# The first two pairs of output blocks of a fused kernel's third matrix product also in seven half-products, their steps interleaved

## The chip, the cores and the metric

The kernel runs on one core of a Trainium2 chip. The metric is the device time of one execution in microseconds (us). TensorE (PE in the profile) multiplies matrices into PSUM banks, VectorE (DVE) and ScalarE (ACT) work elementwise, GpSimd (POOL) helps in the first stage, and SyncE (SP) issues the transfers.

## The reference, cut to what matters

An attention, then two feed-forward layers, all in float32, on 896 tokens (two batches of 448):

```python
x = attention(q, k, v)                                    # 896 x 768
h = np.maximum(np.maximum(x @ w1, x @ w2), x @ w3)        # w1, w2, w3: 768 x 768
y = h @ w_out                                             # 768 x 768
h2 = y @ w_in                                             # 768 x 2048
g = np.where(h2 > 0.0, h2, np.exp(np.minimum(h2, 0.0)) - 1.0)
out = g @ w_out2                                          # 2048 x 768
```

The change touches `y @ w_in`.

## The kernel before, in words

Everything is kept transposed: features on the 128 partitions, the 448 tokens of one batch along the free dimension. A weight block is 128 output columns wide and has six chunks of 128 rows. A float32 number is held as a high and a low part, so one chunk of one block for one batch takes three matmuls of 128x448: high weights by high data, high weights by low data, low weights by high data. A standard block is 2 batches x 6 chunks x 3 = 36 matmuls.

`unit` (called by name from the three matrix stages) does two neighbouring blocks f and f+1 in seven half-products (half of the chunks, one batch; 9 matmuls each) where the standard way has eight. It needs differences of the weights, named 13 and 24 in the program, and sums of the data, `sums_y` with q = 0 to 3, three chunks each. In the order of the code the products of a unit are called here:

- A: first half of block f's weights by the first three chunks of batch 0 (no sums)
- F: weights 13 by sums q=0, put aside as `s5` (function `out5`)
- Q1: weights 24 by sums q=1
- B: second half of block f's weights by the last three chunks of batch 0 (function `second`, no sums)
- Q2: weights 13 by sums q=2
- D: second half of block f+1's weights by sums q=3
- E: weights 24 by the last three chunks of batch 1 (no sums)

ScalarE copies the running PSUM bank aside at three points (`seed`, tiles pgs0, pgs1, pgs2), and VectorE adds `s5` to two of the four results (`added`). The weights reach a unit like this: SyncE loads a raw block (two buffers, `raw_wg`); ScalarE makes `top` (L194, one buffer); VectorE makes the float32 block `b_g` of raw and top (L196, one buffer `ub` for both blocks of a unit); VectorE forms 13 (`f13`, L760) and 24 (two half-size instructions, L777, in place); and `split` makes the high part on ScalarE (`hi`, L743) and the low part on VectorE (`lo`, L202) of each of 0, 13, 24 and 1. There are two buffers for 13 and 24 together (`ul`), and three (`w`) for 0 and 1. Each result then goes through `elu`: Relu and Exp on ScalarE (tile `e`), the join on VectorE (`gf`, L1019), and the split of g into a high part (ScalarE, L1024) and a low part (VectorE, L167).

Stage by stage: attention; h (tiles ph, p, ps); y in six standard blocks in the order `PY` (tiles py0, py1 for the two batches, L930 and L934); then w_in in 16 blocks (tiles pg): blocks 0 and 1 standard, the other seven pairs (2, 4, ... 14, `PG_UNITS`) as units one after the other in the order A, F, Q1, B, Q2, D, E; then out (tiles po). `y_block` splits y on ScalarE and VectorE (tiles x), and `y_sums` forms the sums of a chunk pair when both of its y blocks are there (VectorE steps `spare`, L978 and L990, and a split of each, tiles s and c).

The order of the instructions on each engine is written by a planner (`Plan.order` with `late_plan`): each task has an engine, an estimated cost and a due time `at`; the order in which TensorE's products are given is fixed by the code (`on_pe`), the other engines' order follows from the due times and the planner's estimates.

Of the kernel before, what the change touches and what calls it, by code (L numbers as in the profile page):

```python
# [8 lines left out]
F32 = mybir.dt.float32  # L9
# [11 lines left out]
B, H, S, D = 2, 12, 448, 64  # L21
# [19 lines left out]
PG_UNITS = (2, 4, 6, 8, 10, 12, 14)  # L41
PO_UNITS = (2,4,)
PO_CUT = 6
AWAY = 4
# [113 lines left out]
def fused_kernel(ctx: ExitStack, tc: tile.TileContext, qk, v, w1, w2, w3, wo, wi2, wo2, outT):  # L158
# [553 lines left out]
    def unit(name, src, lean, left, sums, leave, kind="p", base=0, stops=False):  # L712
# [76 lines left out]
        split("24", tk, "t", at + 2400, [t4, opened], slice(0, NK), [(u, name, 3)] if lean else [ut])  # L789
        split(1, None, "w", at + 9000, [full[1], ready["24"] if stops else None], dn, [(u, name, 3)])  # L790

        def product(ps, what, k, xs, after, q=None, gives=(), new=False):

            def run(eng):
# [12 lines left out]
                run, 9, [ready[what], *after] + ([sums.made[q, c] for c in range(HALF)] if q is not None else []),  # L807
# [24 lines left out]
        t5 = product(p, "13", 0, None, [], q=0, new=True)  # L832
        spare = "s5" if not lean else "best1" if kind == "po" else "ot"

        def out5(eng):
            pool, tag = {"s5": (pools.get("s5"), "s5"), "best1": (bp, "best1"), "ot": (pools.get("ot"), "ot")}[spare]
            s5.append(pool.tile([128, S], F32, tag=tag, name=f"s5_{name}"))
            nc.scalar.copy(s5[0], p[0])

        t5 = task(out5, "ACT", 530, clock[0] + 2000, [t5], takes=[spare], gives=["m"])  # L840
        yield
        t = product(a, "24", 0, None, [sb], q=1)
        sd = seed(a, d, t)
        yield
        if not stops:
            second()
            yield
# [150 lines left out]
    for f in PY:  # L998
        y_block(f, py_banks if PG_UNITS else None)
        if f >= HALF and PG_UNITS:  # L1000
            y_sums(f - HALF, py_banks)
# [46 lines left out]
    f = 0  # L1048
    while f < NF:
        if f in PG_UNITS:  # L1050

            def leave_g(k, b, ps, after, gives, at, more=None, frees=()):
                if more is not None:
                    after = [*after, added(ps, more, after, at, frees)]
                elu(f + k, b, ps, after, at, gives)

            list(unit(f"g{f}", [wi2[f], wi2[f + 1]], True, y, sums_y, leave_g, "pg"))
            f += 2
            continue
        parts, t = load(wi2[f], f"wi2_{f}", clock[0])  # L1060
        ps = [[] for _ in range(B)]

        def product(eng, chunks, ps=ps, parts=parts, f=f):
            if chunks[0] == 0:
                for b in range(B):
                    ps[b].append(psum(f"pg{f}_{b}"))
            multiply(ps, parts, y, 0, NK, True, True, chunks)
# [76 lines left out]
    f = 0  # L1144
# [68 lines left out]
```

## Time and profile before

| | |
|---|---|
| median of three runs | 459.61 us (459.44 to 460.14) |
| the profiled execution, its own time | 459.15 us |
| its span in the trace | 457.40 us |
| instructions | 6818 |
| TensorE matmuls | 2456 |
| busy: PE, DVE, ACT, POOL | 451.0, 349.0, 304.2, 43.0 us |

Busy time is the time in which an engine works on instructions. All times below are counted from the start of the span; 1.75 us of the execution's time lie outside it. A matmul's end is modelled (362 ns shown for each, while they start every 200 ns), so starts are what to read on TensorE.

### The profile page before, as it was taken

Reading aid. Unit: us, or ns where it says so; the run is one execution under the profiler, and the core shown is the slowest. Engines: PE = TensorE matmul, PEld = TensorE weight load, DVE = VectorE, ACT = ScalarE, POOL = GpSimd, SP = SyncE. Lnnn points to the kernel's source line nnn. Section 1 sums busy time; section 2 is a strip of 40 time slices with the busy share of each in tenths; the row PEclk is TensorE's granted clock in tenths of the full one; section 3 lists DMA queues with packets and bytes.
Section 4 is the critical chain, followed back from the end, with each engine's and each line's share of the span. In section 5 each row is a group of like instructions: output and inputs, shape, how many; then the busy total and the mean of one; then the engine's idle time right before and its main releaser. Section 6 shows DMA issues by size and latency. Waiting matters only on the chain.

```text
span 457.4 us, 6818 instructions
## 1 busy us (share of the span) xinstructions
PE 451.0 (99%) x2456; PEld 397.5 (87%) x2456; DVE 349.0 (76%) x696; ACT 304.2 (67%) x610; POOL 43.0 (9%) x93
## 2 busy tenths in 40 slices
PE   7999999999999999999999999999999999999996
PEld 3657657799999999999999999999999999999996
DVE  4999898589889994577689699999999797363201
ACT  5999897585666874354647799999995446443200
POOL 4665473000000000000000000000000000000000
PEclk9999999999999999999999999999999999999999
DMA  6463521244225531132341754233459425643002
GB/s 212 165 215 112 183 62 42 120 167 179 94 74 187 199 138 70 70 139 69 138 154 55 300 194 142 107 134 138 138 178 374 139 74 191 195 173 126 1 1 80
DMA packets 16273, 63.22 MB, mean 138 GB/s; under 512 B 1776, under 2 KB 3824, under 8 KB 16240
## 3 DMA queue, kind: packets, MB, share of 16 engines
q1 hardware_dynamic: 16240, 62.79, 39.5%
q8 instruction: 19, 0.31, 0.3%
q14 instruction: 14, 0.11, 0.1%
HBM read 56.36 MB, written 6.42 MB: 137 GB/s over the span
## 4 chain that ended last, share of the span: by engine, by line
PE 93%; DVE 2%; ACT 2%; DMA 1%; POOL 1%; issue 0%; SPq 0%; ACTq 0%
PE p L802 11%; PE pg00g L802 8%; PE ps L802 8%; PE py L930 6%; PE po L930 6%; PE pt L389 4%; PE o L412 4%; PE s L342 3%; PE py L934 3%; PE po L934 3%; PE pgs1g L802 3%; PE pgs0g L802 3%; PE pgs2g L802 3%; PE pg130g L802 3%; PE po00o L802 2%; PE ph L223 2%
## 5 line engine op out<-in xcount | busy, mean ns | idle before, releaser
L366 ACT ACTIVATE pr<-pr,nmx 128x384 f32<-128x384 f32 (+2 forms) x72 | 35.9, 504 | 4.4 <-DVE nmx L356 4.3
L930 PE MATMUL py<-h,hi_wo 128*128 128x448 f32 x144 | 34.6, 362 | 0.0
L194 ACT ACTIVATE top<-raw_wo 128x768 f16<-128x768 bf16 (+1 forms) x24 | 24.2, 1009 | 14.9 <-DMA raw_wo<-in_wo 9.2
L214 ACT ACTIVATE hi_wo<-f_wo 128x768 fp32r<-128x768 f32 (+1 forms) x20 | 15.7, 785 | 25.1 <-PE po00o L930 8.2
L379 POOL TENSOR_SCALAR pr<-pr,r 128x384 f32<-128x384 f32 (+2 forms) x60 | 29.6, 513 | 23.1 <-DVE r L375 12.5
L356 DVE CUSTOM_DVE_ANT_0 pr<-s,mask 128x384 f32<-128x384 f32 (+2 forms) x72 | 26.7, 414 | 6.3 <-PE s L342 6.1
L202 DVE SCALAR_TENSOR_TENSOR lo_wo<-f_wo,hi_wo 128x768 fp32r<-128x768 f32 (+1 forms) x20 | 17.5, 875 | 18.2 <-ACT hi_wo L214 18.0
L930 PEld LDWEIGHTS py<-h,hi_wo 128*128 128x128 f32 x144 | 27.0, 188 | 1.8
L342 PE MATMUL s<-qk 64*128 64x384 f32 (+3 forms) x192 | 26.6, 441 | 1.7 <-DMA qk<-in_qk 1.3
L342 PEld LDWEIGHTS s<-qk 64*128 64x128 f32 (+1 forms) x192 | 13.8, 172 | 11.8 <-DVE nmx L356 4.4
L802 PE MATMUL p<-s,hi 128*128 128x448 f32 x84 | 23.6, 362 | 0.0
L802 PE MATMUL ps<-x,hi 128*128 128x448 f32 x84 | 23.6, 362 | 0.0
L389 PE MATMUL pt<-ident,pr 128*128 128x128 f32 x144 | 22.0, 280 | 0.3 <-DVE l L370 0.2
L412 PE MATMUL o<-th,v 128*64 128x448 f32 (+2 forms) x144 | 22.0, 440 | 0.0
L815 ACT COPY ps<-p 128x448 f32<-128x448 f32 x21 | 10.9, 520 | 16.6 <-PE p L802 16.6
L389 PEld LDWEIGHTS pt<-ident,pr 128*128 128x128 f32 x144 | 15.9, 140 | 6.5 <-issue 2.3
L194 ACT ACTIVATE top<-raw_w 128x768 f16<-128x768 bf16 x18 | 19.5, 1083 | 2.1 <-DVE b L196 2.1
L934 PE MATMUL py<-h,lo_wo 128*128 128x448 f32 x72 | 20.2, 362 | 0.0
L194 ACT ACTIVATE top<-raw_wg 128x768 f16<-128x768 bf16 x14 | 15.2, 1085 | 7.5 <-issue 3.3
L802 PE MATMUL pg00g<-s,hi_g 128*128 128x448 f32 x70 | 19.7, 363 | 0.0
L196 DVE SCALAR_TENSOR_TENSOR f_wo<-raw_wo,top 128x768 int32<-128x768 int32 (+1 forms) x20 | 17.5, 874 | 2.4 <-ACT top L194 2.1
L1015 ACT ACTIVATE e<-e 128x448 f32<-128x448 f32 x32 | 18.6, 580 | 0.8
(286 smaller groups left out, 1335.8 us busy)
## 6 DMA issues: line engine op xcount, KB each, us to landing
raw_w<-in_w SPq DMA_DIRECT2D x18, 768.0 KB, 4.4
raw_wo<-in_wo SPq DMA_DIRECT2D x18, 768.0 KB, 4.4
raw_wg<-in_wi SPq DMA_DIRECT2D x14, 768.0 KB, 4.4
qk<-in_qk SPq DMA_DIRECT2D x11, 448.0 KB, 4.1
kept<-h SPq DMA_DIRECT2D x8, 448.0 KB, 2.6
v<-in_v SPq DMA_DIRECT2D x12, 256.0 KB, 3.1
raw_wo<-in_wo SPq DMA_DIRECT2D x6, 512.0 KB, 3.8
out_t<-ot SPq DMA_DIRECT2D x12, 224.0 KB, 2.0
```

The lines of the kernel that those rows point to most:

```text
L194: nc.scalar.mul(spread.bitcast(F16)[:, 1::2], top.bitcast(BF16), -1.0)
L196: nc.vector.scalar_tensor_tensor(out=f(), in0=below, scalar=13, in1=spread, op0=ALU.logical_shift_right, op1=ALU.bitwise_or)
L342: nc.tensor.matmul(out, us[e]["qk"][own, 0, C * i:w], us[e]["qk"][own, 1, :w], start=True, stop=True, skip_group_check=True)
L356: nc.vector.tensor_tensor_reduce(out=pr, in0=u["s", g][j or 0][:, at:at + w], in1=mask_r if i == NB else mask[:, FULL - w:], scale=-0.125, ...
L366: nc.scalar.activation(pr, pr, AF.Exp, bias=u["nmx"][:, n:n + 1], scale=-1.0, accum_out=u["l"][:, n:n + 1])
L379: engines[eng].tensor_scalar(out=u["pr", j, i], in0=u["pr", j, i], scalar1=u["r"][:, n:n + 1], scalar2=1.0, op0=ALU.mult, op1=ALU.mult)
L389: nc.tensor.transpose(pt[:e - C * c, at:at + C], u["pr", j if j is None else j ^ odd, i][:, C * c:e], ident)
L412: nc.tensor.matmul(u["o"][D * j:D * (j + 1), C * c:], u["v"][:, j, c], u["th_r"][:, j ^ odd] if c == NB else u["th"][:, c, j ^ odd, C * c: ...
L802: nc.tensor.matmul(ps[0], wt[:, HALF * kk + c], w[:, i, :], start=(new and c == m == 0), stop=(c == HALF - 1 and m == 2), skip_group_check ...
L930: nc.tensor.matmul(p[0], hi[:, c, :], xs[j][c0 + c][:, i, :], start=first and c == 0 and i == 0, stop=False, skip_group_check=True)
L934: nc.tensor.matmul(p[0], lo[:, c, :], xs[j][c0 + c][:, 0, :], start=False, stop=last and c == n - 1, skip_group_check=True)
L1015: nc.scalar.activation(made["e"], made["e"], AF.Exp, scale=-1.0)
```

## The change

Blocks 0 to 3 are no longer two standard blocks and a unit of blocks 2 and 3: they are two units, g0 (blocks 0 and 1) and g2 (blocks 2 and 3), whose products are interleaved by `G_ORDER`. The order on TensorE is g0's A, g2's A, g0's B, F and Q1, g2's B, g0's Q2, D and E, then g2's Q1, F, Q2, D and E (`late5` puts F behind Q1). B stands early (`stops`), the split of block half 1 waits for 24 (`stops`), and the products on plain data wait for y chunk by chunk (`made`). The due time of the split of 24 is 600 behind a unit's start where it was 2400, in every unit of the kernel; in g2 it is 0. The constant `PG_UNITS` and the standard path of the stage go.

```diff
-PG_UNITS = (2, 4, 6, 8, 10, 12, 14)
+G_ORDER = (0, 1, 0, 0, 0, 1, 0, 0, 0, 1, 1, 1, 1, 1)
...
-    def unit(name, src, lean, left, sums, leave, kind="p", base=0, stops=False):
+    def unit(name, src, lean, left, sums, leave, kind="p", base=0, stops=False, late5=False, made=None):
...
-        split("24", tk, "t", at + 2400, [t4, opened], slice(0, NK), [(u, name, 3)] if lean else [ut])
+        split("24", tk, "t", at + (0 if late5 else 600), [t4, opened], slice(0, NK), [(u, name, 3)] if lean else [ut])
...
-                run, 9, [ready[what], *after] + ([sums.made[q, c] for c in range(HALF)] if q is not None else []),
+                run, 9, [ready[what], *after] + (
+                    [sums.made[q, c] for c in range(HALF)] if q is not None else
+                    [made[xs[0], xs[1] + c] for c in range(HALF)] if made else []),
...
-        t5 = product(p, "13", 0, None, [], q=0, new=True)
+        def fifth():
+            t = product(p, "13", 0, None, [], q=0, new=True)
...
-        t5 = task(out5, "ACT", 530, clock[0] + 2000, [t5], takes=[spare], gives=["m"])
-        yield
+        if not late5:
+            t5 = fifth()
+            yield
         t = product(a, "24", 0, None, [sb], q=1)
         sd = seed(a, d, t)
         yield
+        if late5:
+            t5 = fifth()
+            yield
...
-    f = 0
-    while f < NF:
-        if f in PG_UNITS:
...
-            list(unit(f"g{f}", [wi2[f], wi2[f + 1]], True, y, sums_y, leave_g, "pg"))
-            f += 2
-            continue
-        parts, t = load(wi2[f], f"wi2_{f}", clock[0])
...
+    def g_unit(f, **more):
...
+        return unit(f"g{f}", [wi2[f], wi2[f + 1]], True, y, sums_y, leave_g, "pg", **more)
+
+    two = [g_unit(0, stops=True, made=y_done), g_unit(2, stops=True, late5=True, made=y_done)]
+    for k in G_ORDER:
+        next(two[k])
+    for f in range(4, NF, 2):
+        list(g_unit(f))
```

**VectorE where y ends.** Both programs, from the second raw block of pair 2 and 3 (`b_g2`) on; `py0_5` and `py1_5` are the last y block's banks, `spare` the sums, x5, x11 and s0_2 the low parts. Before:

```order
L196 SCALAR_TENSOR_TENSOR b_g2_2723<-raw_wg2_1_2694,top0_70 128x768
L760 TENSOR_TENSOR f13_g2_2754<-b_g2_2723 128x768
L978 TENSOR_TENSOR spare1_2785<-spare0_2726,py1_5_2697 128x448
L978 TENSOR_TENSOR spare3_2788<-spare1_2785,py0_2_2634 128x448
L990 TENSOR_TENSOR spare0_2726<-py0_5_2696,spare3_2788 128x448
L167 TENSOR_TENSOR x5_922<-py0_5_2696,x5_922 128x448
```

With the change:

```order
L196 SCALAR_TENSOR_TENSOR b_g2_2746<-raw_wg2_1_2637,top0_70 128x768
L760 TENSOR_TENSOR f13_g2_2775<-b_g2_2746 128x768
L777 TENSOR_TENSOR b_g2_2746<-b_g2_2746,f13_g2_2775 128x384
L202 SCALAR_TENSOR_TENSOR lo0_g2_2778<-b_g2_2746,hi0_g2_2777 128x768
L777 TENSOR_TENSOR b_g2_2746<-b_g2_2746 128x384
L988 TENSOR_TENSOR spare1_2799<-spare0_2735,py1_5_2704 128x448
L988 TENSOR_TENSOR spare3_2802<-spare1_2799,py0_2_2640 128x448
L1000 TENSOR_TENSOR spare0_2735<-py0_5_2703,spare3_2802 128x448
L167 TENSOR_TENSOR x5_922<-py0_5_2703,x5_922 128x448
```

Three instructions on g2's weights now stand ahead of the last sums.

**ScalarE from the split of g2's 13 to the second raw block of unit g4**, with the change (`e` are Relu and Exp of results, `pgs1g2` a copied bank, `s5_g2` the product F put aside):

```order
L743 ACTIVATE hi13_g2_2922<-f13_g2_2775 128x768
L1025 ACTIVATE e1_1_2910<-e1_1_2910 128x448
L1022 ACTIVATE e1_0_2929<-pgs1g0_2861 128x448
L1025 ACTIVATE e1_0_2929<-e1_0_2929 128x448
L817 COPY pgs1g2_2946<-pg00g2_2789 128x448
L1034 CAST h1_1_1381<-gf1_1_2934 128x448
L1034 CAST h0_1_1375<-gf1_0_2948 128x448
L1022 ACTIVATE e0_1_2953<-pgs2g0_2890 128x448
L1025 ACTIVATE e0_1_2953<-e0_1_2953 128x448
L841 COPY s5_g2_2967<-pg130g2_2936 128x448
L194 ACTIVATE top0_70<-raw_wg4_1_2780 128x768
```

Before, the `top` of that raw block stood eight instructions ahead of the copy `s5_g2`:

```order
L743 ACTIVATE hi1_g2_2875<-b_g2_2723 128x384
L1024 CAST h1_0_1380<-gf0_1_2873 128x448
L194 ACTIVATE top0_70<-raw_wg4_1_2756 128x768
L1012 ACTIVATE e1_0_2900<-pg1_0_2822 128x448
L1015 ACTIVATE e1_0_2900<-e1_0_2900 128x448
L1012 ACTIVATE e1_1_2905<-pg1_1_2823 128x448
L1015 ACTIVATE e1_1_2905<-e1_1_2905 128x448
L815 COPY pgs0g2_2922<-pg00g2_2889 128x448
```

So the second raw block of g4 is now taken behind g2's F; before, it was taken ahead of g2's first copied bank (`pgs0g2`).

**VectorE behind that `top`**, with the change, up to the low part of g4's 13:

```order
L196 SCALAR_TENSOR_TENSOR b_g4_2925<-raw_wg4_1_2780,top0_70 128x768
L167 TENSOR_TENSOR h1_0_1380<-gf0_1_2969,h1_0_1380 128x448
L1054 TENSOR_TENSOR pg00g2_2789<-pg00g2_2789,s5_g2_2967 128x448
L760 TENSOR_TENSOR f13_g4_3005<-b_g4_2925 128x768
L202 SCALAR_TENSOR_TENSOR lo0_g4_2987<-b_g4_2925,hi0_g4_2986 128x768
L777 TENSOR_TENSOR b_g4_2925<-b_g4_2925,f13_g4_3005 128x384
L1029 SCALAR_TENSOR_TENSOR gf3_1_3027<-e3_1_3009,pg00g2_2789 128x448
L777 TENSOR_TENSOR b_g4_2925<-b_g4_2925 128x384
L202 SCALAR_TENSOR_TENSOR lo13_g4_3025<-f13_g4_3005,hi13_g4_3024 128x768
```

Before, the low part of g4's 0 (`lo0_g4`) stood ahead of the add on `pg00g2`; now it stands behind it.

## Rows read from the trace of the kernel before

**Rows 1.** The page: busy time of each engine; transfers of raw blocks.

```profile
PE 451.0 (99%) x2456; PEld 397.5 (87%) x2456; DVE 349.0 (76%) x696; ACT 304.2 (67%) x610; POOL 43.0 (9%) x93
...
raw_wg<-in_wi SPq DMA_DIRECT2D x14, 768.0 KB, 4.4
```

**Rows 2.** Waits of TensorE, the longest of its four rows (total us, times, longest).

```profile
PE s L342 <- DMA qk<-in_qk: 1.3, 1, 1.3
```

**Rows 3.** Windows: PE, PEld, DVE, ACT, POOL busy (instructions), PEclk, DMA share, GB/s.

```profile
240.00:254.00 14.00, 14.00 (x72) 13.14 (x71) 12.00 (x20) 9.88 (x18) 0.00 (x0) 1.00 0.30 114
...
305.00:317.00 12.00, 12.00 (x62) 11.27 (x61) 11.75 (x19) 11.68 (x22) 0.00 (x0) 1.00 0.37 133
```

**Rows 4.** Timeline of TensorE, end of y to unit g4: start, us, line, op.

```profile
239.55 0.96 PE L930 MATMUL pg<-x,hi_wi 128*128 128x448 f32 x4
...
253.95 0.56 PE L802 MATMUL pg00g<-x,hi_g 128*128 128x448 f32 x2
254.35 0.36 PE L802 MATMUL pg00g<-x,lo_g 128*128 128x448 f32 x1
...
255.75 0.56 PE L802 MATMUL pg130g<-s,hi_g 128*128 128x448 f32 x2
...
268.35 0.56 PE L802 MATMUL pg130g<-s,hi_g 128*128 128x448 f32 x2
```

**Rows 5.** Timeline of DVE, last y blocks and unit g2 (in brackets: idle before, releaser).

```profile
225.35 1.27 DVE L978 TENSOR_TENSOR spare<-spare,py 128x448 f32<-128x448 f32 x2 [2.01 <-PE py L934]
...
233.07 0.96 DVE L196 SCALAR_TENSOR_TENSOR b_g<-raw_wg,top 128x768 int32<-128x768 int32 x1 [1.20 <-ACT top L194]
...
237.47 0.96 DVE L196 SCALAR_TENSOR_TENSOR b_g<-raw_wg,top 128x768 int32<-128x768 int32 x1 [0.44 <-ACT top L194]
...
239.75 1.27 DVE L978 TENSOR_TENSOR spare<-spare,py 128x448 f32<-128x448 f32 x2 [0.33 <-PE py L934]
...
241.79 1.15 DVE L167 TENSOR_TENSOR x<-py,x 128x448 fp32r<-128x448 f32 x2
242.88 1.16 DVE L167 TENSOR_TENSOR s<-spare,s 128x448 fp32r<-128x448 f32 x2
...
244.49 0.95 DVE L202 SCALAR_TENSOR_TENSOR lo_g<-b_g,hi_g 128x768 fp32r<-128x768 f32 x1
245.36 0.55 DVE L777 TENSOR_TENSOR b_g<-b_g,f_g 128x384 f32<-128x384 f32 x1
...
265.49 0.95 DVE L202 SCALAR_TENSOR_TENSOR lo_g<-f_g,hi_g 128x768 fp32r<-128x768 f32 x1
```

**Rows 6.** Timeline of ACT in a later unit.

```profile
300.95 0.52 ACT L815 COPY pgs2g<-pg00g 128x448 f32<-128x448 f32 x1 [0.23 <-PE pg00g L802]
301.38 0.85 ACT L743 ACTIVATE hi_g<-f_g 128x768 fp32r<-128x768 f32 x1
302.13 0.55 ACT L1024 CAST c<-gf 128x448 fp32r<-128x448 f32 x1
302.58 0.55 ACT L1012 ACTIVATE e<-pg00g 128x448 f32<-128x448 f32 x1
303.15 0.58 ACT L1015 ACTIVATE e<-e 128x448 f32<-128x448 f32 x1
303.64 1.08 ACT L194 ACTIVATE top<-raw_wg 128x768 f16<-128x768 bf16 x1
304.58 0.83 ACT L743 ACTIVATE hi_g<-b_g 128x768 fp32r<-128x768 f32 x1
...
306.82 0.53 ACT L815 COPY pgs0g<-pg00g 128x448 f32<-128x448 f32 x1
307.28 0.53 ACT L1012 ACTIVATE e<-pgs2g 128x448 f32<-128x448 f32 x1
...
308.65 0.52 ACT L838 COPY s_g<-pg130g 128x448 f32<-128x448 f32 x1
309.07 1.09 ACT L194 ACTIVATE top<-raw_wg 128x768 f16<-128x768 bf16 x1
```

More of the change, by code (lines that the diff above doesn't have):

```diff
@@ L831, in unit, with out5 @@
             yield
-        t5 = product(p, "13", 0, None, [], q=0, new=True)
-        spare = "s5" if not lean else "best1" if kind == "po" else "ot"
[L835 to L838, printed above, removed]
-        t5 = task(out5, "ACT", 530, clock[0] + 2000, [t5], takes=[spare], gives=["m"])
-        yield
+        def fifth():
+            t = product(p, "13", 0, None, [], q=0, new=True)
+            def out5(eng):
+                pool, tag = {"s5": (pools.get("s5"), "s5"), "best1": (bp, "best1"), "ot": (pools.get("ot"), "ot")}[spare]
+                s5.append(pool.tile([128, S], F32, tag=tag, name=f"s5_{name}"))
+                nc.scalar.copy(s5[0], p[0])
+            return task(out5, "ACT", 530, clock[0] + 2000, [t], takes=[spare], gives=["m"])
+        spare = "s5" if not lean else "best1" if kind == "po" else "ot"
+        if not late5:
+            t5 = fifth()
+            yield
         t = product(a, "24", 0, None, [sb], q=1)
@@ L998, in fused_kernel @@
     for f in PY:
-        y_block(f, py_banks if PG_UNITS else None)
-        if f >= HALF and PG_UNITS:
+        y_block(f, py_banks)
+        if f >= HALF:
             y_sums(f - HALF, py_banks)
@@ L1046, in added, with leave_g @@
         return task(both, "DVE", 619, at, after, gives=gives)
-    f = 0
-    while f < NF:
-        if f in PG_UNITS:
[L1052 to L1055, printed above, removed]
-            list(unit(f"g{f}", [wi2[f], wi2[f + 1]], True, y, sums_y, leave_g, "pg"))
-            f += 2
-            continue
-        parts, t = load(wi2[f], f"wi2_{f}", clock[0])
[L1061 to L1067, printed above, removed]
-        groups = ((0, 1, 3, 4), (2, 5)) if f == 0 else (tuple(range(NK)),)
-        for chunks in groups:
-            t = on_pe(lambda eng, c=chunks, p=product: p(eng, c), 6 * len(chunks),
-                      [t, *(y_done[b, c] for c in chunks for b in range(B))],
-                      takes=["m", "m"] * (chunks[0] == 0), gives=["w"] * (chunks is groups[-1]))
-        for b in range(B):
-            elu(f, b, ps[b], [t], clock[0] + 3000, ["m"])
-        f += 1
+    def g_unit(f, **more):
+        def leave_g(k, b, ps, after, gives, at, more=None, frees=()):
+            if more is not None:
+                after = [*after, added(ps, more, after, at, frees)]
+            elu(f + k, b, ps, after, at, gives)
+        return unit(f"g{f}", [wi2[f], wi2[f + 1]], True, y, sums_y, leave_g, "pg", **more)
[4 more added lines that the diff above has]
+        list(g_unit(f))
     for f in range(AWAY):
```

## The prediction

> **What bounds the kernel now.** First the page: TensorE is busy 451.0 of 457.4 us [rows 1]. Then its waits: four rows, the longest 1.3 us and on the first loads, none on a weight block, a sum or a y block [rows 2]. Then the windows: in the stretch of the standard blocks and in a unit's, TensorE is busy all the time, at a granted clock of 1.00, while VectorE and ScalarE have 2.0 and 4.1 us left of 14 in the first and about 0.3 of 12 in the second [rows 3]. So a matmul less is 200 ns less as long as the weights and sums keep arriving ahead of TensorE, and the two other engines have little left with which to keep that up.
>
> **The matmuls.** The standard pair starts at 239.55 and unit g2 at 253.95: 72 matmuls in 14.40 us, 200 ns each. A half-product of nine takes 1.80 (253.95 to 255.75), a unit 12.60 (F of g2 at 255.75, F of g4 at 268.35) [rows 4]. The pair becomes 63 matmuls: **9 x 0.200 = 1.80 us less**. The rows say 200 ns per start at clock 1.00. The Trainium skill ("TensorE: Matmul & The Clock Gate", section "Wait — 56ns, not 53.3ns?") gives columns over 2.4 GHz plus about 2.5 ns, which for 448 columns would be 189 ns, a gain of 1.70 and a forecast 0.1 us higher; the measured 200 decides.
>
> Without waits the products of g0 and g2 start every 1.80 from 239.55: A, A of g2, B (243.15), F (244.95), Q1, B of g2, Q2, D, E (253.95 to 255.75), then g2's Q1, F, Q2, D, E, and g4's A at 264.75 and F at 266.55 (before: 266.55 and 268.35). Each wait below is taken against this list. A product's third matmul, 0.40 after its start, is the first that needs the low part of the weights: each chunk takes two matmuls with the high weights and then one with the low [rows 4].
>
> **What VectorE and ScalarE get.** Back to back a 128x448 instruction of VectorE takes 0.53 (two in 1.15, the last one 0.62 to its end), a 128x768 one 0.87, a half-size one 0.5 [rows 5]. The unit in place of the standard pair adds two low parts and f13 (2.6), two half-size differences (1.0) and two adds (1.1), and halves one low part (-0.4): 4.3 us. ScalarE gets two high parts more (1.5), four copies (1.8), and one half-size high part (-0.3): 3.0. The four raw blocks, their `top` and their 4.4 us transfers [rows 1] stay four; they are issued when buffers come free.
>
> **The last sums.** Before, 14.40 us of standard products stood between y and the first sum; now A, A and B, 5.4 us. VectorE works without other waits than three on `top` and on y from 225.35 to 239.75: 1.20, 0.44 and 0.33 us idle [rows 5]. In that stretch it gets two low parts and two half-size differences of g0 more (2.7), a smaller low part (-0.4) and one block less (-0.9); g2's two differences and its low part of 0 stand ahead of the last sums (1.9). That is 3.3 us of work against 2.0 of idle time, and the wait for the second `top` (1.09 long, 0.5 of it covered) may stay: the sums start 1.3 to 2.1 late, at 241.1 to 241.9. Before, the low part of x5 was there 2.66 after that start (241.79 + 0.62) and that of s0_2 3.75 after (242.88 + 0.62) [rows 5]: now by 244.5 and 245.6 at the latest. B needs x5 at its eighth matmul, 244.55, F needs s0_2 at 246.35. **No wait; upper bound 0.2.** ScalarE's high part of g2's 0 takes the weight buffer that the last y block frees at about 239.35, so its cast of x5 comes at 240.1, still ahead of VectorE. The first raw block of g4 is issued at about 236.8, when `b_g2` has been read, lands at 241.2, and ScalarE wants it at 242.0: no wait. The stores of the first results now stand ahead of g6's raw blocks on SyncE; those are wanted from 264 on and issued by 263, 4.4 us ahead of the later one's use at 272: nothing.
>
> **The weights of g4: the term that decides.** The interleaving spends g2's A and B early. So only five products (9.00 us) stand between E of g0 and A of g4, where a later unit has seven, yet ScalarE and VectorE have a unit's whole work between them. The chain: the high part of g2's 13 needs the buffer that E of g0 frees with its eighth matmul. Its 0.20 end at 255.55, and ScalarE starts 0.2 behind that: Q2 of g8, three products behind an F at 255.75 + 3 x 12.60, is over at 300.75, and the copy `pgs2g` that waits for it starts at 300.95 [rows 4, 6]. So 255.75. From there ScalarE is busy by the order shown: high 0.75, Exp 0.49, Relu 0.57, Exp 0.49, copy 0.46, two casts 0.90, Relu 0.57, Exp 0.49, copy `s5` 0.42, `top` 1.09 [rows 6] = 6.23. VectorE then: block 0.87, low part 0.53, add 0.53, f13 0.87, low part of 0 0.95 = 3.75. The low part stands at 265.73; A of g4 needs it at 265.15: **0.6 us of waiting**, 0.7 with a handover of 0.1. Behind it: half-size difference, join, half-size difference and the low part of 13, from 264.78 on 0.87 + 0.5 + 0.53 + 0.5 + 0.95, done at 268.13; F of g4 needs it at 266.95. That is 1.2, or 1.3 with the handover: **another 0.6**. For the handover no row of this stage shows a price, since nothing waits here now; bounds 0 and 0.2, from the idle time behind a release in rows 5 and 6 (0.2 to 0.3 with the producer's own tail in it), and I take 0.1. Before, this low part was started at 265.49 for an F at 268.35 [rows 4, 5], 2.9 us ahead: that is the cover that goes.
>
> **The later units.** Their order changes with the due time of 24. I follow E of a unit (its end seen at T) to F two units on: ScalarE Relu, cast, high part of 24, then the copy that waits for A (T + 1.80), and behind it copy 0.46, Exp 0.49, `top` 0.94, Relu 0.57, Exp 0.49, cast 0.45, `s5` 0.42, copy 0.46, `top` 1.09 [rows 6]: T + 7.2. VectorE: block, low part, f13, join, add, low part of 0, low part, difference, join, difference, low part of 13: 7.2. Sum T + 14.4; TensorE is there at T - 0.20 + 12.60 + 1.80 + 0.40 = T + 14.6. It just fits: **0, with 0.2 to spare**, in five units. What follows (out) has seconds of cover by count: VectorE's busy share falls behind g14, and I cost its one-place shifts at nothing.
>
> **Sum.** -1.80 + 0 + 0.7 + 0.6 + 0 = **-0.5 us**, from 459.15 of the profiled execution to 458.65. That execution lies 0.46 below the median of 459.61, so against the median: **459.1 us**.
>
> **Rivals.**
> 1. *Nothing waits*: 459.61 - 1.80 = 457.8. For it: not one wait of this stage in the trace of before, and the two chains of g4 consist of ten and more small terms; 0.1 less on each of four ScalarE steps and the wait in A goes, and VectorE's part follows. Against it: the pitches are those of a full ScalarE, they vary by 0.02. It decides (over 0.2%, 0.92 us) when the waits sum to under 0.9. Chance 0.29.
> 2. *The ring of the later units is longer than TensorE's 12.60*: then each of the five units g6 to g14 waits, since E is late by it and the next ring starts from there. Its slack is 0.2; three handovers at 0.2 make the ring 15.0, 0.4 too long: 5 x 0.4 + 1.3 = 3.3 of waits, 459.61 - 1.8 + 3.3 = **461.1**. It is slower by over 0.2% from 0.28 per unit on. For it: ScalarE has 0.3 of 12 us left [rows 3], and the weight order loses 2 us of lead. Against it: in a ring every term is a measured pitch with the handover between ScalarE and VectorE in it. Chance 0.14.
> 3. *The sums come late*: VectorE another 2.5 later (a raw block that lands late would do that, through `top`), F waits 2.0, and g4's waits remain: 461.1. The transfers are issued earlier than before, which speaks against. Chance 0.03.
>
> That the change does less than it says is excluded by the order: 63 matmuls stand where 72 stood.
>
> **How the numbers follow.** The forecast, waits between 0.9 and 2.7 in sum, has 0.54, and stays within 0.2% (0.92 us, about what the measurement can tell from no change). Faster 0.29 (rival 1), slower 0.17 (rivals 2 and 3). The range takes in rival 1 and the forecast with its bounds (handovers 0 to 0.2, the 0.2 in B, 0.1 to 0.2 in each later unit): 457.6 to 460.6. Left out are most of rivals 2 and 3.
>
> **What would show it.** In the profile after: 2447 matmuls; g0's A at 239.55; g4's A and F with idle time of TensorE ahead of their third matmul, released by VectorE's low part (`lo_g`), together 1.3; no such row at B or F of g0; at most 0.2 in each later F; clock 1.00. No row of TensorE's waits in this stage means rival 1. Rows of about equal size in every unit mean rival 2, and a wait on a sum rival 3. A wait elsewhere would make the forecast wrong in its mechanism even if the time fits.

## The result, and the profile after

| | before | after |
|---|---|---|
| median | 459.52 us (459.39 to 460.14, four runs) | 464.99 us (464.88 to 466.31, four runs) |
| ratio, 95% interval | | 1.0125 (1.0107 to 1.0143) |
| the profiled execution, its span | 459.15, 457.4 us | 464.96, 463.1 us |

The change made the kernel **5.5 us slower**. The forecast was 459.1 (457.6 to 460.6), and slower had been given a chance of 0.17.

The page after, busy time by engine, beside [rows 1]:

```profile
PE 456.6 (99%) x2447; PEld 395.0 (85%) x2447; DVE 351.6 (76%) x703; ACT 307.8 (66%) x616; POOL 42.8 (9%) x93
```

Nine matmuls fewer, as forecast, and TensorE is busy 5.6 us longer. So most of the loss is not idle time. The waits of the weight loads (PEld) in the timeline from 240 us on (only the rows with idle time are shown; in brackets the idle time and what ended it):

```profile
242.71 0.19 PEld L802 LDWEIGHTS pg00g<-x,lo_g 128*128 128x128 f32 x1 [0.47 <-DVE lo_g L202]
245.67 0.19 PEld L802 LDWEIGHTS pgs0g<-x,hi_g 128*128 128x128 f32 x1 [0.26 <-DVE x L167]
259.14 0.19 PEld L802 LDWEIGHTS pg130g<-s,lo_g 128*128 128x128 f32 x1 [0.16 <-DVE lo_g L202]
267.04 0.19 PEld L802 LDWEIGHTS pg00g<-x,lo_g 128*128 128x128 f32 x1 [0.78 <-DVE lo_g L202]
269.38 0.19 PEld L802 LDWEIGHTS pg130g<-s,lo_g 128*128 128x128 f32 x1 [0.63 <-DVE lo_g L202]
282.04 0.19 PEld L802 LDWEIGHTS pg130g<-s,lo_g 128*128 128x128 f32 x1 [0.15 <-DVE lo_g L202]
294.71 0.19 PEld L802 LDWEIGHTS pg130g<-s,lo_g 128*128 128x128 f32 x1 [0.16 <-DVE lo_g L202]
```

They are A of g2, B of g0, F of g2, A and F of g4, F of g6 and of g8; F of g10 follows below. In the kernel before there is no such row. Now the windows, two stretches behind all this, first of the kernel before, then of the changed one (columns as in [rows 3]):

```profile
343.00:380.00 37.00, 37.00 (x187) 34.73 (x186) 32.73 (x54) 19.47 (x33) 0.00 (x0) 1.00 0.57 202
380.00:430.00 50.00, 50.00 (x252) 46.94 (x251) 24.54 (x32) 22.69 (x32) 0.00 (x0) 1.00 0.43 142
```

```profile
343.00:380.00 37.00, 37.00 (x180) 33.48 (x180) 33.34 (x55) 18.98 (x33) 0.00 (x0) 1.00 0.60 213
380.00:430.00 50.00, 50.00 (x243) 45.24 (x243) 23.75 (x32) 23.85 (x34) 0.00 (x0) 1.00 0.48 158
```

TensorE is busy all the time in both, at a granted clock of 1.00 in both, and starts 243 matmuls where it started 252. **The matmuls themselves stand further apart.** The timeline of TensorE shows where that begins, at F of g10:

```profile
306.82 0.36 PE L802 MATMUL pg00g<-x,lo_g 128*128 128x448 f32 x1
307.02 0.56 PE L802 MATMUL pg130g<-s,hi_g 128*128 128x448 f32 x2
307.42 0.43 PE L802 MATMUL pg130g<-s,lo_g 128*128 128x448 f32 x1
307.69 0.57 PE L802 MATMUL pg130g<-s,hi_g 128*128 128x448 f32 x2
308.10 0.37 PE L802 MATMUL pg130g<-s,lo_g 128*128 128x448 f32 x1
308.31 0.57 PE L802 MATMUL pg130g<-s,hi_g 128*128 128x448 f32 x2
308.72 0.37 PE L802 MATMUL pg130g<-s,lo_g 128*128 128x448 f32 x1
```

Up to 307.42 a group of three takes 0.60 us. The low part of 13 comes 0.07 late, so the matmul behind it starts at 307.69, and from there on a group takes 0.62. It stays so through the rest of pg and all of out: 734 distances of 206.67 ns, to the last matmul. Before, all 1816 distances from 90.35 to 453.55 us are 200.00.

With the start times one can put each profiled execution together: the time at which the even run of matmuls begins, 200 ns for each matmul, what single distances have over 200 (the waits), and 6.67 ns for each matmul of a stretch at 206.67. For the changed kernel: the even run begins at 91.04 and not at 90.35 (+0.69; nothing is changed up to there, and over the profiles below it begins between 90.27 and 93.13); nine matmuls fewer (-1.80); waits +2.04; 734 x 6.67 ns (+4.89). Sum +5.8, against spans of 463.1 and 457.4.

### The profile page after: what moved, and what is told of

Its sections match the earlier page's. It is cut to its first block, busy times and chain, and to the rows that moved or that the text cites. A ratio compares the mean times of both kernels' runs of the same rounds, so it can differ in the third digit from the quotient of the medians.

```text
span 463.1 us, 6808 instructions
## 1 busy us (share of the span) xinstructions
PE 456.6 (99%) x2447; PEld 395.0 (85%) x2447; DVE 351.6 (76%) x703; ACT 307.8 (66%) x616; POOL 42.8 (9%) x93
## 4 chain that ended last, share of the span: by engine, by line
PE 84%; DVE 6%; ACT 5%; DMA 2%; issue 1%; POOL 1%; SPq 0%; ACTq 0%; DVEq 0%
PE p L802 11%; PE ps L802 8%; PE pg00g L802 8%; PE po L940 6%; PE pt L389 4%; PE o L412 4%; PE s L342 3%; PE pgs0g L802 3%; PE po L944 3%; PE pg130g L802 3%; PE pgs1g L802 3%; PE pgs2g L802 3%; PE po00o L802 2%; PE ph L223 2%; PE py L940 2%; PE ph L226 2%
## 5 line engine op out<-in xcount | busy, mean ns | idle before, releaser
L342 PE MATMUL s<-qk 64*128 64x384 f32 (+3 forms) x192 | 27.9, 447 | 1.2 <-DMA qk<-in_qk 1.1
L802 PE MATMUL pg00g<-s,hi_g 128*128 128x448 f32 x80 | 22.7, 364 | 0.0
L194 ACT ACTIVATE top<-raw_wg 128x768 f16<-128x768 bf16 x16 | 17.3, 1082 | 7.0 <-issue 3.3
L202 DVE SCALAR_TENSOR_TENSOR lo_g<-b_g,hi_g 128x768 fp32r<-128x768 f32 (+1 forms) x24 | 19.6, 816 | 0.7 <-ACT hi_g L743 0.7
L196 DVE SCALAR_TENSOR_TENSOR b_g<-raw_wg,top 128x768 int32<-128x768 int32 x16 | 15.3, 958 | 6.0 <-ACT top L194 5.5
```

Of the source, the lines that this page charges most:

```text
L194: nc.scalar.mul(spread.bitcast(F16)[:, 1::2], top.bitcast(BF16), -1.0)
L202: nc.vector.scalar_tensor_tensor(out=lo, in0=f, scalar=-1.0, in1=hi.bitcast(F32), op0=ALU.mult, op1=ALU.subtract)
L342: nc.tensor.matmul(out, us[e]["qk"][own, 0, C * i:w], us[e]["qk"][own, 1, :w], start=True, stop=True, skip_group_check=True)
L802: nc.tensor.matmul(ps[0], wt[:, HALF * kk + c], w[:, i, :], start=(new and c == m == 0), stop=(c == HALF - 1 and m == 2), skip_group_check ...
```

## The experiments

Two theories say why the matmuls stand further apart. **P**: a wait, or any break, sets the distance of the matmuls behind it. **C**: something that does not depend on waits slows TensorE. Two more say where the waits come from. **A**: ScalarE is full (it is busy 25.13 of the 25.50 us from 279.5 to 305.0). **V**: VectorE is (24.42).

This is what the profiles showed, worked out from the start times as above (time and waits in us; an added matmul counts among the waits). The code shown with each run is condensed to what differs.

| run | its time | even run from | waits | matmuls at 206.67 |
|---|---|---|---|---|
| before | 459.15 | 90.35 | 0 | 0 |
| after | 464.96 | 91.04 | 2.04 | 734 |
| e1 | 462.20 | 91.10 | 3.03 | 100 |
| e2 | 460.84 | 92.03 | 0 | 0 |
| e5 | 462.51 | 91.16 | 3.15 | 184 |
| e6 | 463.23 | 93.13 | 2.48 | 100 |
| e7 | 466.99 | 90.39 | 1.71 | 915 |
| e9 | 460.48 | 90.97 | 2.31 | 0 |
| e10 | 464.51 | 90.42 | 3.96 | 471 |
| e11 | 466.04 | 90.27 | 2.96 | 811 |
| e12 | 464.13 | 90.70 | 6.25 | 27 |
| e13 | 465.50 | 91.14 | 2.60 | 723 |
| e15 | 460.75 | 91.25 | 0.67 | 0 |
| e16 | 460.33 | 90.52 | 2.45 | 59 |
| e17 | 464.44 | 91.11 | 5.13 | 184 |

Two rows hold something else. In e6 the even run begins 2.8 us later than in the kernel before; the granted clock was 0.50 from 8.4 to 11.7 us there, where the kernel before had 1.00. In e17, 1.59 of the 5.13 us are no wait: right behind a wait of 2.6 us ten matmuls stand up to 374 ns apart at the lower of the two clock levels (1.2 GHz):

```profile
270.70:273.90 3.20, 3.20 (x10) 2.83 (x10) 0.46 (x1) 0.27 (x1) 0.00 (x0) 0.50 0.00 0
```

Behind the last matmul each span has 3.8 us more (4.0 in e9, 4.2 in e1 and e11).

### The matmuls alone: e4, e8, e14

```diff
+for i in range(64):                        # e4
+    for c in range(10):
+        matmul(ps, hi[:, c % 6], xr[:, 0]); matmul(ps, hi[:, c % 6], xr[:, 1])
+        matmul(ps, late if c == 0 else lo[:, c % 6], xr[:, 0])
+    # VectorE: 7 full operations, one of 256 + 16 * i columns, then late
```

> Not the reference's computation: the matmuls alone, 64 stretches of 30 matmuls of the same form (128x448, each with its own weight load), and from the third on the third weight load of a stretch waits on a chain of VectorE operations that is 16 elements (some 17 ns) longer from one stretch to the next, so that the wait grows from nothing to about 0.7 us. Theory P: the distance of the matmuls within a stretch is set by the wait at its start and holds for the whole stretch: 200.0 ns after most waits, 206.7 after some, and while nothing waits it stays what it was. Theory C (the engine is slowed by something that does not depend on waits, such as its clock): the distance is the same after every wait, or changes in the middle of stretches.

Measured: while nothing waits, 25 stretches at 206.7. From the first wait on, 38 stretches: 6 at 206.7 and 32 at 202.6 to 202.7 on average (a pattern of 207, 202, 203, 202 or 203, 199), each held to the next wait. TensorE's timeline over one such wait (L108 `lt` is the matmul that waits):

```profile
191.04 0.36 PE L106 MATMUL ps<-xr,hi 128*128 128x448 f32 x1
...
194.69 0.36 PE L106 MATMUL ps<-xr,hi 128*128 128x448 f32 x1
...
195.50 0.36 PE L107 MATMUL ps<-xr,hi 128*128 128x448 f32 x1
195.70 0.46 PE L108 MATMUL ps<-xr,lt 128*128 128x448 f32 x1
196.00 0.36 PE L106 MATMUL ps<-xr,hi 128*128 128x448 f32 x1
...
196.61 0.37 PE L106 MATMUL ps<-xr,hi 128*128 128x448 f32 x1
...
200.95 0.37 PE L106 MATMUL ps<-xr,hi 128*128 128x448 f32 x1
```

Ahead of it 18 distances in 3.65 us, behind it 21 in 4.34: 202.8 and 206.7 ns. So theory C falls: the same matmuls change their distance at a wait, and not in between. What stands at 200.0 in the kernel alternates around 202.7 here, and no run shows why; the longer distance is the same in both.

e8 puts a narrow matmul of other weights ahead of each stretch in place of the wait, 20, 24, ... 268 columns wide (e14: 386, 388, ... 510):

```diff
+    matmul(ps[:, :16 + 4 * i], ones, ones_row[:, :16 + 4 * i])   # e14: 384 + 2 * i
```

> Not the reference's computation: the matmuls alone as in the run with the growing waits, 64 stretches of 30 matmuls with no wait anywhere; instead, each stretch but the first begins with one narrow matmul of other weights, 20 columns wide in the second stretch and 4 columns wider in each that follows. Theory P as it stands after that run (what counts is where the starts of the matmuls stand against a raster of 6.67 ns, and a wait only moves them on it): the distance within a stretch changes from stretch to stretch here too, 206.7 after some widths and 200 to 203 after others, without a wait; a shift by a multiple of 16 columns keeps a stretch of 206.7 as it was. Theory W (it takes a wait on a semaphore): 206.7 in all 64 stretches, as in the 25 that came before the first wait there.

59 of 63 stretches at 202.6 to 202.7, four at 206.7 (widths 108, 124, 260 and 268), with no semaphore waited for: **it takes a break, not a semaphore**. TensorE's timeline around the first of the four (L103 is the narrow matmul):

```profile
146.01 0.36 PE L108 MATMUL ps<-xr,lo 128*128 128x448 f32 x1
...
151.49 0.36 PE L108 MATMUL ps<-xr,lo 128*128 128x448 f32 x1
151.69 0.22 PE L103 MATMUL ps<-const-bfloat16-1.0 128*128 128x108 bf16 x1
...
152.23 0.37 PE L108 MATMUL ps<-xr,lo 128*128 128x448 f32 x1
...
157.81 0.37 PE L108 MATMUL ps<-xr,lo 128*128 128x448 f32 x1
```

27 distances take 5.48 us ahead of it and 5.58 behind it. But 59 is no rate at which a break ends the longer distance: here the first stretch already stands at 202.7 (in e4 it stands at 206.7), so most breaks kept what they found. Four began 206.7, and the three that came upon it ended it. The width itself did not matter: from the narrow matmul's start to that of the second matmul behind it are 0.323 to 0.330 us, whether it has 20 or 268 columns, so no rule of 16 could be seen. e14 takes widths whose time counts:

> Not the reference's computation: the run with the narrow matmuls once more, with wide ones: each stretch of 30 matmuls but the first begins with a matmul of other weights that is 386 columns wide in the second stretch and 2 columns wider in each that follows, up to 510. Theory R (raster): a start that is moved by a whole number of 6.67 ns (16 columns) keeps 206.7, so in a row of widths 206.7 comes back every 16 columns, that is every eighth stretch, and the others stand at 200 to 203. Theory N (no rule that the width sets): 206.7 in some of the 63 stretches at irregular widths, or in none.

| width of the first matmul | distance behind it |
|---|---|
| 386, 388 | 206.7 |
| 410, 426, 442, 458, 474, 490, 506 | 206.7 |
| the other 54, 390 to 510 | 202.6 to 202.7 |

From 398 on, where the time of the break grows with the width (0.385 to 0.433 us, some 6.7 ns per 16 columns), theory R holds: 206.7 came at every sixteenth column, seven times out of seven at a remainder of 10 (by 16), and at none of the other 50 widths. Below that the break takes 0.377 to 0.380 whatever the width, and the rule does not hold: 386 (remainder 2) began 206.7, 388 carried it on, and 394 (remainder 10) did not begin it. All seven began it out of a stretch at 202.7, and the next width (remainder 12) ended it each time; what a multiple of 16 does to a stretch at 206.7 is not in this run.

### The kernel before, disturbed: e7, e15

```diff
-                nc.scalar.mul(hl[what][0][:, sl], fs[what][:, sl], -1.0)
+                for _ in range(4 if (name, what) == ("g4", "13") else 1):
+                    nc.scalar.mul(hl[what][0][:, sl], fs[what][:, sl], -1.0)
```

> The kernel before, nothing interleaved and all its products in place, with ScalarE held for 2.55 us in g4: the high part of 13 is computed four times. Theory A: F has 2.1 us to spare there; now F of g4 waits 0.4 us, the lead does not come back because ScalarE has 12.66 us of work per unit, and F waits some 0.06 us in most later units; 459.4 + 0.4 + 0.3 = 460.1 with the pace at 200.00. Theory P: each of these waits can leave 206.67, and then the kernel before loses as the changed one did: 462 to 465. Theory I (it is the interleaving, the new order of products and banks, that slows the later units): waits or not, no matmul stands 206.67 apart, and the time is 460.1 at most.

466.76 (466.10 to 467.65), ratio 1.0157 (1.0141 to 1.0173). The timeline of TensorE shows one wait, not at F but at the next product, on a copy of ScalarE's:

```profile
270.00 0.36 PE L803 MATMUL pg130g<-s,lo_g 128*128 128x448 f32 x1
271.79 0.67 PE L803 MATMUL pg00g<-s,hi_g 128*128 128x448 f32 x2 [1.43 <-ACT pgs0g L816]
272.30 0.37 PE L803 MATMUL pg00g<-s,lo_g 128*128 128x448 f32 x1
272.50 0.57 PE L803 MATMUL pg00g<-s,hi_g 128*128 128x448 f32 x2
272.92 0.37 PE L803 MATMUL pg00g<-s,lo_g 128*128 128x448 f32 x1
```

and the windows 14 us ahead of it, 14 us behind it and late in the kernel:

```profile
255.00:269.00 14.00, 14.00 (x72) 13.12 (x71) 9.10 (x15) 12.47 (x22) 0.00 (x0) 1.00 0.48 192
273.00:287.00 14.00, 14.00 (x70) 12.66 (x69) 12.90 (x21) 13.59 (x25) 0.00 (x0) 1.00 0.56 184
...
380.00:430.00 50.00, 50.00 (x244) 45.24 (x243) 25.74 (x34) 23.98 (x35) 0.00 (x0) 1.00 0.49 158
```

A wait of 1.6 us costs 7.8 in the profiled execution: 1.7 by itself and 915 x 6.67 ns = 6.1 behind it. Nothing is interleaved here, so theory I (of the expectation above) falls, and P is shown in the kernel before. A's small waits in the later units did not come; at 206.67 a unit takes 13.0 us, and ScalarE keeps up.

e15 adds five narrow matmuls to the kernel before:

```diff
+                if new and what == "13" and name in ("g10", "g12", "g14", "o2", "o4"):
+                    nc.tensor.matmul(ps[0][:, :64], ones, ones_row[:, :64], start=True, stop=True, ...)
```

> The kernel before with the five narrow matmuls of 64 columns that were added to the changed one (before the first matmul of F in g10, g12, g14 and of the two pairs of the output); no wait is added and no wait was there. Theory P: five breaks without a wait; each costs 0.13 us, and any of them can leave 206.67 for all that follows: 460.2 in the executions where none does, 463 to 465 where one in g10 to g14 does, both seen over the executions. Theory W (it takes a wait): 460.2 in all, 200.0 throughout.

460.31 (459.57 to 461.83), 200.0 throughout in the profile. The five cost what was expected and changed no distance. By itself that would speak for W, but in e8 breaks without a wait begin 206.7. That the break has a fixed length here, 327 ns or 49 x 6.67, and so carries on what it finds, is argued and not shown: in e8 three breaks of about that length (324 to 328 ns) ended 206.7.

### The due time alone: e2, e1

```diff
-        split("24", tk, "t", at + 2400, [t4, opened], ...)   # before, e2
+        split("24", tk, "t", at + 600, [t4, opened], ...)
-        split("24", tk, "t", at + (0 if late5 else 600), ...)   # after, e1
+        split("24", tk, "t", at + (0 if late5 else 2400), ...)
```

> The kernel before with that part alone: the parts of 24 are due at 600 and not at 2400, nothing interleaved. Theories P and A: lo13 had 2.1 to 2.3 us to spare at F in the kernel before, so F waits nowhere, the pace stays at 200.00 and the time at 459.5 (within 0.3). Theory D: 461 or more, with waits at F.

459.72 against 459.36, ratio 1.0003 (0.9991 to 1.0015), no wait: the due time alone does nothing.

> The changed kernel with one part undone: the low and high parts of 24 of the ordinary units are due at 2400 again, not at 600; the first two pairs stay interleaved. Theory P (pace): of the 5.5 us that the change lost, 4.9 come from 734 matmuls that stand 206.67 ns apart and not 200.00, from 307.4 us to the end, and this pace began at a short wait of TensorE on a weight's low part (product F of g10, 70 ns). If the earlier due time makes those waits, they go here, no matmul stands 206.67 apart, and the time is 464.99 - 4.9 - 0.3 (the waits of F in g6 to g12 with it) = 459.8. Theory A (ACT is full): ACT works 12.66 us per unit without a pause against 12.60 of TensorE, whatever the due time, so the waits of some 60 ns in each unit stay; then the pace after each of them decides, and the time is 460.1 if none of them sets the longer one, 464 to 465 if one does again. Theory D (the due time alone costs, by the order on DVE): below 460 with the pace at 200.00 and no waits at F.

462.20 (461.34 to 462.49 in five runs, 466.47 and 466.52 in two). The waits became more, 3.03 us, so the due time of 600 was not what made them. 206.67 held for 100 matmuls from B of g0 on and ended at A of g4, where TensorE waited: the second of the two bunches of times may be executions in which 206.67 held to the end, but only one of the first was profiled.

### The changed kernel with more breaks: e6, e13, e16

e6 computes two thirds of the low part of 13 in g12 twice:

```diff
+                if (name, what) == ("g12", "13"):
+                    rest(hl[what][1][:, :4], fs[what][:, :4], hl[what][0][:, :4])
```

> The changed kernel with one more wait: before the low part of 13 in g12 VectorE computes two thirds of it a first time (some 0.7 us), so that F of g12 waits for some 0.3 us at about 320 us. Theory P: the distance, 206.67 from g10 on, is set anew there; after most waits of the run of matmuls alone (31 of 37) it was not the longer one, so most likely 200.0 for the 673 matmuls that are left, and the time falls by 4.5 and rises by the wait of 0.3, to 460.8: a longer wait makes the kernel faster. If it stays at 206.67 after this wait: 465.0 to 465.3. Theory C (the engine is slowed by something else from 307 us on): 465.3 with 206.67 to the end.

465.27 (463.23 to 466.47), profiled at 463.23: no fall. In that execution F of g10 had left 200.0, so there was nothing to end; the stretch at 206.67 stood earlier, 248 to 269 us, begun by B's wait and ended by A's of g4. **The same program draws differently from one execution to the next.** e13 adds the five narrow matmuls of e15:

> The changed kernel with five matmuls more that compute nothing: one of 64 columns of a constant before the first matmul of F in g10, g12, g14 and of the two pairs of the output, into the bank that F then starts anew. Nothing is taken away, and every wait of the changed kernel stays. Theory P: each of the five moves the starts of the matmuls, as in the run with the narrow matmuls, and ends a stretch of 206.67 in most cases (59 of 63 there); they cost some 0.13 us each; 464.99 - 4.9 + 0.7 + 0.4 = 461.2: work that is added makes the kernel faster by 3.8. If the longer distance has another cause: 464.99 + 0.7 = 465.7.

463.3: six runs at 459.8 to 461.9, six at 464.7 to 466.1. The profiled one is of the second bunch: 206.67 began at the narrow matmul of g10 and was carried over the four others. My expectation that each break draws anew was wrong, and so was the 59 of 63 that it rested on (e8). e16 takes 448 columns, a multiple of 16, ahead of F in g12, g14 and o2:

```diff
+                if new and what == "13" and name in ("g12", "g14", "o2"):
+                    nc.tensor.matmul(ps[0], ones, ones_row[:, :S], start=True, stop=True, ...)
```

> The changed kernel, every wait left in place, with three matmuls more that compute nothing: 448 columns of a constant, before the first matmul of F in g12, in g14 and in the first pair of the output. In the run with the wide matmuls a width that is a multiple of 16 was followed by the shorter distance in all 8 cases, and 206.7 was carried on at a remainder of 4 and begun at a remainder of 10 only. Theory R: 206.67 from F of g10 or earlier ends at 320 or 333 us at the latest and does not come back in the output stage; the three cost 0.2 us each; 464.99 - 4.9 + 0.6 + 0.4 (63 matmuls at 206.67 from g10 to g12) = 461.1, in nearly all executions (one in which a wait in g12 or g14 sets it anew is ended by the third, with 0.8 more). Theory N (another cause beside the distance): 465.6 in most.

**461.14** (460.33 to 464.33; seven of nine within 460.33 to 462.65), expected 461.1: 3.9 us less than the changed kernel by work that is added, with its waits in place. The time fits, but the profiled execution shows what was expected at one of the three only. The wait at F of g10 left 200.0 there, so there was nothing to end; 206.67 begins right behind the wide matmul of g12, where no weight load waits for another engine, and ends at the one of g14; the one of o2 keeps 200.0. So the same width began the longer distance once and ended it once, against the expectation (the widths of e14 that are multiples of 16 were seven, not eight, and each stood behind a stretch at 202.7). That the wide matmuls shortened the other eight executions in this way is likely from the times, and not shown. Timeline and windows around the wide matmul of g14 (L800):

```profile
331.54 0.57 PE L806 MATMUL pg00g<-x,hi_g 128*128 128x448 f32 x2
331.95 0.36 PE L806 MATMUL pg00g<-x,lo_g 128*128 128x448 f32 x1
332.15 0.36 PE L800 MATMUL pg130g<-const-bfloat16-1.0 128*128 128x448 bf16 x1
332.19 0.73 PE L806 MATMUL pg130g<-s,hi_g 128*128 128x448 f32 x2
332.76 0.36 PE L806 MATMUL pg130g<-s,lo_g 128*128 128x448 f32 x1
332.96 0.56 PE L806 MATMUL pg130g<-s,hi_g 128*128 128x448 f32 x2
333.36 0.36 PE L806 MATMUL pg130g<-s,lo_g 128*128 128x448 f32 x1
```

```profile
320.00:332.00 12.00, 12.00 (x60) 10.82 (x58) 11.45 (x19) 11.39 (x21) 0.00 (x0) 1.00 0.40 131
333.00:345.00 12.00, 12.00 (x62) 11.27 (x61) 10.88 (x18) 11.72 (x21) 0.00 (x0) 1.00 0.46 136
```

### Taking the waits away: e9, e5, e10, e11, e12, e17

None of these beat the kernel before. e9:

```diff
-        t = task(exp, "ACT", 570, at, [t])
```

> The changed kernel without the exponential of the activation (32 operations of ScalarE of 0.58 us each left out, four per unit; the negative side of the output is not the reference's). Theory A: ScalarE has 10.3 us of work per unit and its lead stays, so A and F of g4 and F of g6 to g14 wait for nothing; the waits of g2's A and F and of g0's B on the low parts and sums just before (0.5 us in all) may stay. Theory P: what the last of these waits leaves decides: 457.8 + 0.5 = 458.3 at 200.00, up to 464 at 206.67, and a mix over the executions if it differs from one to the next. Theory V (VectorE alone makes F late): VectorE has the same work, so the waits in g4 and later stay, 459.4 or more even at 200.00.

460.39 (459.72 to 462.13). The waits, 2.31 us, are no shorter: F of g4, g6, g10 and g14 waits for VectorE. So theory A as the sole cause falls: ScalarE is busy 53.1 of the 64 us from 270 to 334. V is not shown by it either. VectorE is busy 60.5 of them and stands idle 0.66 us in each unit for a `top` of ScalarE's (0.45 to 0.60 in the changed kernel). That is more than F loses in g4, g10 and g14 (0.34 to 0.45) and nearly what it loses in g6 (0.75). So the low part seems late through both engines and their order, and not through the load of one; no run here separates the two. The profile has no stretch at 206.67, and the time is that of the waits alone.

e5 and e10 give one cast in four to GpSimd, planned at 1.0 and at 1.9 us:

```diff
-            nc.scalar.copy(g[b][f][:, 0], made["f"])
+            (nc.gpsimd.tensor_copy if (f % 2, b) == (1, 1) else nc.scalar.copy)(g[b][f][:, 0], made["f"])
```

> The changed kernel with one of the four casts of a unit (ScalarE, 0.55 us, the high part of the second block's second half) done by GpSimd, which is idle in this stage. Theory A (ScalarE is full: 12.66 us of work per unit against TensorE's 12.60, and the 2.1 us of lead that it had at g4 in the kernel before went into the first two pairs): with 12.1 us per unit there is no wait at F in g6 to g14, and the two waits in g4 (0.57 and 0.42 us) become short or go; the waits on the sums and on low parts in g0 and g2 (0.8 us in all) may stay. Theory P (a wait sets the distance of the matmuls after it): after the last wait it is 200.00 or 206.67 to the end; 464.99 - 4.9 - 1.3 = 458.8 with the first, 463 to 465 with the second. Theory V (VectorE is the one that is late, and GpSimd disturbs it): waits at F as in the changed kernel or longer, 465 or more.

> The changed kernel with the cast on GpSimd again, but the planner is told that it takes 1.9 us (it was told 1.0 and it took 1.64 to 1.70 beside VectorE), so that the subtraction that needs it stands later on VectorE, where it had waited 0.46 us for it in every unit. Theory A: no waits of F in the later units now; 458.8 if the last wait leaves 200.00, 463 to 465 if it leaves 206.67. Theory V: VectorE stays late, waits in every unit, 461 or more at either distance.

463.15 and 463.30. In e5 VectorE stood 0.46 us per unit for the cast; in e10 no longer, but the low part of 13 beside it took 1.32 for 0.95, and F waited 0.6 in several units (VectorE's timeline):

```profile
293.36 0.56 DVE L777 TENSOR_TENSOR b_g<-b_g 128x384 f32<-128x384 f32 x1
293.83 1.32 DVE L202 SCALAR_TENSOR_TENSOR lo_g<-f_g,hi_g 128x768 fp32r<-128x768 f32 x1
295.07 0.62 DVE L1056 TENSOR_TENSOR pgs1g<-pgs1g,s_g 128x448 f32<-128x448 f32 x1
295.60 0.94 DVE L202 SCALAR_TENSOR_TENSOR lo_g<-b_g,hi_g 128x768 fp32r<-128x768 f32 x1
```

e11, e12 and e17 move the weights of g4 ahead and the differences for 24 of g2 back; e11 and e12 use GpSimd too (casts as in e5, subtractions alike), e17 the wide matmuls of g14 and o2:

```diff
-        at = clock[0]
+        at = clock[0] - early          # 4000 in g4, else 0
-            t2 = task(less_in(dn, ...), "DVE", 555, at, [t1])
+            t2 = task(less_in(dn, ...), "DVE", 555, at + (1500 if late5 else 0), [t1])   # t4 alike
```

> The changed kernel with what makes TensorE wait taken away: in blocks 0 to 11 of pg one cast in four (ScalarE's) and one subtraction in four (VectorE's) go to GpSimd, the weights of g4 are due 4 us earlier, and the two subtractions for 24 of g2 are due 1.5 us later, behind the last sums. Theory P with the waits as the cause: A and F of g4 and F of the later units no longer wait, nor B of g0; A and F of g2 may still wait, 0.5 to 0.9 us in all; then 459.4 - 1.8 + 0.7 = 458.3 in the executions where the last wait leaves 200.00, and up to 464 in those where it leaves 206.67, so most of the times near 458.3. Theory L (the longer distance comes with the seven products for all pairs, waits or not): 463 or more although the waits are gone.

> As the run before it, with two casts and two subtractions of each unit on GpSimd instead of one of each. Theory P: if one of each was enough, the same time within 0.3 (458.3); if waits were left in the later units, they go now, and it is the faster one. Rival: GpSimd, which took 1.7 us for a cast beside VectorE, becomes the engine that is late; then the low parts of the activation come late and the output stage waits at its start, 459 or more.

> The changed kernel with two of these matmuls (F of g14 and of the first pair of the output), and with two due times moved on the engines that convert weights, without GpSimd: the weights of g4 are due 4 us earlier, and the two subtractions for 24 of g2 1.5 us later, behind the last sums. If that takes away the waits of A and F of g4 and of B of g0 as intended: 459.4 - 1.8 + 0.8 (A and F of g2, F of g6 to g12) + 0.4 + 0.3 = 459.1 with the shorter distance, 460 where 206.67 holds for some units. If the earlier weights of g4 push the activation back instead, so that F finds no bank free, as in the run with GpSimd and the due times: 461 or more.

466.71, 465.49 and 464.13. All three met the same new wait: the activation now stands behind the weights of g4 on VectorE, and F of g4 waits 1.9 to 2.6 us for a bank. The waits of TensorE's loads from 240 to 345 us in e11:

```profile
PEld pg130g L802 <- DVE gf L1029: 1.9, 1, 1.9
PEld pg00g L802 <- ACT pgs1g L817: 0.8, 1, 0.8
PEld pg00g L802 <- DVE lo_g L202: 0.3, 1, 0.3
PEld pg130g L802 <- DVE lo_g L202: 0.3, 1, 0.3
```

B of g0 waits no more, as intended. e17's wide matmul ended a stretch of 184 matmuls at 336.3. e12 had only two short stretches at 206.67, 27 matmuls together (0.18 us), and lost by its waits, 6.25.

## Why the prediction was wrong

- **The matmuls**: 63 for 72, 1.80 us less: right. "A matmul less is 200 ns less as long as the weights and sums keep arriving" was right too, but the other half of it, that a matmul *is* 200 ns whatever happens, was not. Of the Trainium skill's rule that I weighed there ("TensorE: Matmul & The Clock Gate", section "Wait — 56ns, not 53.3ns?": columns over 2.4 GHz and a fixed cost of about 2.5 ns), no row shows the 189 ns that one estimates from it; the rows show 200.0 and 206.7, at one clock.
- **The last sums**: no wait forecast, at most 0.2; B waited 0.16 on x5. Within the bound.
- **What was not in the list**: A of g2 needed its low part at 242.44 and lost 0.38. I had that low part on VectorE only as a delay of the sums and never asked when A itself needs it.
- **The weights of g4**: forecast 0.7 at A and 0.6 at F, on the low part; measured 0.68 and 0.54. The mechanism and the size are right, the handover of 0.1 included: behind each longer wait the next matmul comes 0.31 later, not 0.20.
- **The later units**: 0 to 0.2 forecast; 0.06, 0.06 and 0.07 in g6 to g10.
- **The sum**: waits of 2.04 where I had 1.3, so by its own terms the change gains nothing, +0.2, which is still inside the range. **The step that failed is the sum itself: it priced each wait at its own length.** The last one, 0.07 us long, cost 4.9. In e7 one of 1.6 cost 6.1 more.
- **The rivals**: none was this. Rival 2 has the right place (small waits in every unit) and the wrong price: 0.06 a unit is nothing, what follows is everything. That no later wait ends it fits the mechanism: at 206.67 a unit takes 13.0 us, the other engines get 0.4 more per unit, and the waits that could have set 200.00 again stop.
- **The signs**: "clock 1.00" was listed as a sign that all is well. It cannot tell 200.00 from 206.67; the count of matmuls per window can.
- What the trace of before could have told: nothing of the second distance, since no matmul waits there behind 91 us. It did show that all margins were used up, and that deserved a wider range on the slow side.

How often it strikes stays open for any one place. In the profiled executions of the changed kernel and its versions 12 of 96 waits left the longer distance and 84 the shorter. Eight of the 96 came upon a stretch at 206.67, and all eight ended it. That three of the four runs of the changed kernel lie within 0.13 us speaks for the same place in each, but only one of them was profiled.

## What to carry to other kernels

A kernel whose TensorE never waits is worth more than its idle time shows: a wait, however short, can make every matmul up to the next break slower (here 12 waits of 96 did), so price a new wait in a full TensorE stream by what stands behind it too, and not by its length alone. When a run is slower and TensorE is busy at full clock, count the matmuls per window before looking for waits. If waits can't be avoided, an added matmul behind the last of them can set the shorter distance again (e16: 3.9 us for 0.6), but none of the widths here did so every time: judge it by the times of many executions.

## What the runs showed of the hardware that was not expected

- Matmuls of 128x448, each with its own weight load, have two steady distances at a clock of 1.00: 206.67 ns, and 200.0 (in the matmuls alone 202.7 on average). The difference of 6.67 ns is the time of 16 columns at 2.4 GHz. Which one holds goes with where the starts fall on a raster of 6.67 ns: in e14, from 398 columns on, one width in sixteen columns begins the longer one, and in all eleven profiles of whole kernels that have both, the starts of the two states, taken modulo 6.67 ns, differ by 2.0 to 3.2 ns. What in the chip has this raster no run shows.
- At a granted clock of 0.50 the same matmuls stand 373 to 374 ns apart (e17, 270.7 to 273.9 us).
- A narrow matmul between others costs 0.12 us whether it has 20 or 268 columns (e8), 0.13 in the kernel (e15), and one of 448 columns 0.2 (e16).
- A cast on GpSimd beside VectorE made a VectorE instruction of 0.95 us take 1.32 (e10).
